# Splitting the loads of a large key/value cache over two queues, in place of sixteen tiny loads at the end

## The chip, the cores and the metric

The kernel runs on one core of a Trainium2 chip. The metric is the device time of one execution in microseconds (us), the median of the runs. The core's engines appear in the profile as PE (matrix multiplications; PEld is the loading of its stationary operand), DVE (vector work), ACT (scalar work, activations), POOL and SP (which here only issues transfers). Transfers between the large memory and the on-chip buffer are issued by SP or ACT and carried by 16 DMA engines that the core's queues share.

## What is computed

Two attention blocks for one new token, concatenated. Block A has 32 heads, each with its own keys and values over 32768 positions; block B has 32 query heads over 8 key/value heads and looks at the last 4096 positions only. All inputs are bf16.

```python
# A: x (1,1,512), k_cache and v_cache (1,32,32768,128), wq (512,4096), wo (4096,512)
q = (x @ wq) per head
scores = einsum("bhqd,bhkd->bhqk", q, k_cache) * 128 ** -0.5
p = softmax(scores)
o = einsum("bhqk,bhkd->bhqd", p, v_cache)
a = o @ wo
# B: the same with caches (1,8,32768,128), the last W = 4096 positions,
#    each key/value head used by four query heads
return concatenate([a, b], axis=-1)      # (1,1,1024)
```

A's caches are 2 x 268.4 MB; they are read once and make up 536.9 MB of the 570.4 MB that the kernel reads.

## The kernel before

The work is written as lists of operations, one list for each engine, with the waits between them derived from dependencies (`op`, `emit`). Each engine runs its own list in order. PE and DVE run the 32 heads of A as a loop of 16 passes of two heads; ACT and SP run theirs as straight code.

First come B's two groups of heads (`emit_qproj`, `emit_unit`, `emit_stats`, `emit_PT`, `emit_PV`), whose loads are 4 MB each. Then comes the loop over A's 32 heads (line 381). A head g does this:

- `load_k` (line 314) issues one load of 8 MB: 128 partitions, 64 KB each, into two of the three thirds of `kbuf`; the third of the thirds still holds keys of the head before. The load may start when PE has read the thirds it overwrites. The last head's keys come as two loads of 4 MB.
- `load_v` (line 327) issues one load of 8 MB into `vbuf`, which holds one head only. It may start when PE has finished the head before's product with the values (line 599).
- `emit_qcopy` (line 469): ACT copies the head's query into `qw`.
- `emit_unit` (line 473): PE transposes the keys in 32 batches (line 497), DVE copies each batch out (line 500), PE multiplies with the query (line 519). The first of these products needs `qw`.
- `emit_stats`: the maximum over the scores by DVE and PE, then the exponential on ACT (line 547).
- `emit_PT`: PE transposes the probabilities (line 571), ACT copies them (line 574) and copies a selector `hw` (line 577).
- `emit_PV`: PE multiplies with the values (line 599), and the result is gathered into `psG` (lines 613 to 626).

Every load of caches and weights is issued by SP through `load` (line 287), so they all stand in one queue, in the order in which SP's list has them: keys of head g, values of head g, keys of head g+1 and so on. Only the two loads of x (1 KB each, line 424) are issued by ACT, at the start.

After the last head SP issues the output weights: `kbuf<-wo`, two loads for B and five for A (line 392). Behind them it issues sixteen tiny loads (line 394): load i brings rows 0 to i, 16 bf16 values each, into the buffer `marks`, which nothing reads. Then come the output's two stores (line 668), and SP's list ends with waits for the sixteen tiny loads (line 399) and for the stores (line 401).

Of the kernel before, what the change touches and what calls it, by code (L numbers as in the profile page):

```python
# [3 lines left out]
BF16 = mybir.dt.bfloat16  # L4
# [5 lines left out]
DH = 128  # L10
NQH = 32
STRIPS = 4
HALF = 128
NT = 4
# [38 lines left out]
class _Kernel:  # L53
# [176 lines left out]
    def alloc(self):  # L230
        nc = self.nc
        sb = nc.alloc_sbuf_tensor
        self.kbuf = sb("kbuf", [128, 3 * HALF * DH], BF16)
        self.vbuf = sb("vbuf", [128, 2 * HALF * DH], BF16)
        self.kt = [sb(f"kt{i}", [128, 1024], BF16) for i in range(NKT)]
        self.psb = sb("psb", [128, 512], BF16)
        self.ptsb = sb("ptsb", [128, 512], BF16)
        self.ident = sb("ident", [128, 128], BF16)
        self.ones = sb("ones", [128, 128], BF16)
        self.e32 = sb("e32", [128, 32], F32)  # L240
        self.spread = sb("spread", [32, 4, 128], BF16)
        self.tr = {k: sb(f"tr_{k}", [128, 32], F32) for k in ("in", "a")}
        self.rows64 = sb("rows64", [128, 64], F32)
        self.nscale = sb("nscale", [1, 128], F32)
        self.m4 = sb("m4", [1, 128], F32)
        self.pb = sb("pb", [128, 512], F32)
        self.out_sb = sb("out_sb", [128, 512], BF16)
        self.marks = sb("marks", [16, 17 * 16], BF16)
        self.c = {}
        for name, d in self.X.items():  # L250
            HG = d["HG"]
            self.c[name] = dict(
                x=sb(f"x_{name}", [128, 4], BF16),
                oc=[sb(f"oc_{name}{i}", [128, DH + 1], F32) for i in range(2)],
                b=sb(f"b_{name}", [128, 32], F32),
                cm=sb(f"cm_{name}", [128, 32], F32),
                mr=sb(f"mr_{name}", [1, HG], F32),
                nb=sb(f"nb_{name}", [128, 2], F32),
                hot=sb(f"hot_{name}", [128, d["nb"]], F32),
                lh=sb(f"lh_{name}", [128, HG], F32),  # L260
                hsel=sb(f"hsel_{name}", [128, 64], F32),
                rinv=sb(f"rinv_{name}", [32, 1], F32),
                ob=sb(f"ob_{name}", [32, DH], BF16),
                oz=sb(f"oz_{name}", [128, 32], BF16),
            )

        self.qz = sb("qz", [128, 32 * self.X["B"]["NKVH"] + 64], BF16)
        self.qa = sb("qa", [128, NQH], BF16)
        self.qw = sb("qw", [128, 64], BF16)
        self.hw = sb("hw", [128, 32], F32)  # L270
        ps = nc.alloc_psum_tensor
        self.S = ps("psS", [128, 512], F32)
        self.T = [ps(f"psT{i}", [128, 512], F32) for i in range(NT)]
        self.PT = ps("psPT", [128, 512], F32)
        self.ACC = ps("psACC", [128, 512], F32)
        self.G = ps("psG", [128, 512], F32)
        s = nc.alloc_semaphore
        self.ksem = [s(f"ksem{i}") for i in range(2)]
        self.vsem = [s(f"vsem{i}") for i in range(2)]
        self.xsem = {n: s(f"xsem_{n}") for n in self.X}  # L280
        self.wosem = {n: [s(f"wosem_{n}{i}") for i in range(len(self.WO_CUTS[n]) - 1)] for n in self.X}
        self.outsem = {n: s(f"outsem_{n}") for n in self.X}
        self.marksem = [s(f"marksem{i}") for i in range(16)]

# [24 lines left out]
    def k_thirds(self, g):  # L311
        return (1, 0) if g % 2 == 0 else (1, 2)

    def load_k(self, g, parts):
        w = HALF * DH
        src = self.kv_src("k", "A", g)[:, 0, :]
        lo = min(self.k_thirds(g))
        free = [self.free["k"][t] for t in self.k_thirds(g)]
        if parts == 1:
            self.load(self.kbuf[:, w * lo:w * lo + 2 * w], src, self.mark("k", 0), *free)  # L320
            sem = self.mark("k", 1)
            self.op("sp", lambda e: e.sem_inc(sem, 16))
        else:
            for i, t in enumerate(self.k_thirds(g)):
                self.load(self.kbuf[:, w * t:w * t + w], src[:, w * (t - lo):w * (t - lo) + w], self.mark("k", i), *free)

    def load_v(self, g):
        self.load(self.vbuf[:, :], self.kv_src("v", "A", g)[:, 0, :], self.mark("v", 0), *self.free["v"])

    WQ_SLOT = {"B": 0, "A": 1}  # L330

# [20 lines left out]
    def plan(self):  # L352
        self.lsem = {"k": self.ksem, "v": self.vsem}
        self.fill = {w: [0, 0] for w in "kv"}
        self.free = {"k": [None] * 3, "v": [None] * 2}
        self.nbatch = 0
        self.copies = []
        self.pending = []
        self.psread = self.ptread = self.sread = self.accread = None
        self.gath = self.qcopy = self.hcopy = None  # L360
        self.constants()
        a, b = self.X["A"], self.X["B"]

        self.load_wq("B")
        self.load_b("k", 0)
        self.load_wq("A")
        self.load_b("k", 1)
        self.emit_qproj("B")
        self.emit_unit("B", 0)
        self.emit_qproj("A")  # L370
        self.emit_stats("B", 0)
        self.emit_unit("B", 1, {1: lambda: self.emit_PT("B", 0)})
        self.emit_stats("B", 1)
        for g in range(2):
            if g == 1:
                self.emit_PT("B", g)
            self.load_b("v", g)
            self.emit_PV("B", g)
        self.emit_spread("B")

        for g in range(NQH):
            self.loop = {"pe": g // 2, "dve": g // 2}
            self.load_k(g, 1 if g < NQH - 1 else 2)
            self.load_v(g)
            self.emit_qcopy(g)
            self.emit_unit("A", g)
            self.emit_stats("A", g)
            self.emit_PT("A", g)
            self.emit_PV("A", g)
        self.loop = {}  # L390
        for n in ("B", "A"):
            for part in range(len(self.WO_CUTS[n]) - 1):
                self.load_wo(n, part)
        for i in range(16):
            self.load(self.marks[0:i + 1, 16 * i:16 * i + 16], self.X["A"]["wo"][0:i + 1, 0:16], self.marksem[i])
        self.emit_spread("A")
        self.emit_proj()
        for i in range(16):
            self.op("sp", lambda e, i=i: e.wait_ge(self.marksem[i], 16))
        for n in ("B", "A"):  # L400
            self.op("sp", lambda e, n=n: e.wait_ge(self.outsem[n], 16))

# [70 lines left out]
    def emit_unit(self, name, g, hooks={}):  # L473

        d = self.X[name]
        thirds = (g,) if name == "B" else self.k_thirds(g)
        lo = min(thirds)
        order = [(t, i, 8 * (t - lo) + st) for i, t in enumerate(thirds) for st in range(8)]
        for n, (t, i, st) in enumerate(order):
            for half in range(2):  # L480
                self.emit_T(HALF * lo + 16 * st + 8 * half, self.landed("k", g if name == "B" else i), t)
            if n % 2:
                if n // 2 in hooks:
                    hooks[n // 2]()
                self.pending.append((name, g, order[n - 1][2], n == 1, n == len(order) - 1, self.nbatch - 4))
                if len(self.pending) > 1:
                    self.emit_S(self.pending.pop(0))

    def emit_T(self, tile, landed, third):
        b = self.nbatch  # L490
        self.nbatch += 1
        T, KT = self.T[b % NT][:, :].bitcast(BF16), self.kt[b % NKT]
        src = self.kbuf[:, DH * tile:DH * tile + 1024]
        def tr(e):
            inst = None
            for k in range(8):
                inst = e.transpose(T[:, 128 * k:128 * k + 128], src[:, DH * k:DH * k + DH], self.ident[:, :])  # L497
            return inst
        o = self.op("pe", tr, landed, self.copies[b - NT] if b >= NT else self.k_ident, to="dve")
        self.copies.append(self.op("dve", lambda v: v.tensor_copy(KT[:, :], T[:, :]), o, to="pe"))  # L500
        self.free["k"][third] = o

# [77 lines left out]
    def emit_PV(self, name, g):  # L580
        d, t = self.X[name], self.c[name]
        acc = self.ACC
        pt = self.ptsb[:, :].rearrange("p (j x) -> p j x", x=128)
        if name == "A":
# [3 lines left out]
            rows = 4  # L588
        else:
            w = HALF * DH  # L590
# [4 lines left out]
            rows = 16  # L595
        def mm(e):
# [2 lines left out]
                inst = e.matmul(acc[32 * c:32 * c + rows, 0:512], lhsT=lhsT, rhs=rhs, start=begin, stop=end,  # L599
                                tile_position=(0, 32 * c), skip_group_check=True)  # L600
            return inst
        pv = self.op("pe", mm, self.landed("v", 0 if name == "A" else g), self.ptread, self.accread, to="sp")
        for i in (0, 1) if name == "A" else (g,):
            self.free["v"][i] = pv

        pv = self.emit_gather(name, g, DH, DH + 1)
        oc = t["oc"][g % 2][:, 0:DH]
        o = None
# [101 lines left out]
```

## Time and profile before

| what | value |
|---|---|
| median of 2 runs | 1329.01 us (1328.94 to 1329.09) |
| the profiled execution | 1328.94 us; its span, first to last instruction, 1326.9 us |
| PE busy | 963.9 us, 73% |
| PEld busy | 678.1 us, 51% |
| DVE busy | 749.5 us, 56% |
| ACT busy | 54.8 us, 4% |
| moved by DMA | 570.66 MB, mean 430 GB/s |
| TensorE clock granted, mean | 0.839 of full speed |

Busy shares say how long an engine worked, not whether it set the end. The chain of waits, followed back from the last instruction, says what did. For transfers, the share of a queue is the time that its packets took, as a share of the time of 16 DMA engines. "Us to landing" is the time from a transfer's issue to its completion, and so includes what stood ahead of it.

### The profile page before, as it was taken

What the parts mean: (1) busy time and instruction counts of PE and PEld (TensorE: products, weight loads), DVE (VectorE), ACT (ScalarE), POOL (GpSimd) and SP (SyncE); (2) the same over time, 40 slices, a digit from 0 to 9 for tenths busy, and PEclk for the clock granted to TensorE, in tenths of its full rate; (3) what the DMA queues carried; (4) which work ended last, traced back from release to release, by engine and by line L of the source; (5) the groups of instructions that cost most, each with busy time, mean ns of one, the idle gap of its engine ahead of it and who ended that gap; (6) DMA issues with size and microseconds to landing.
All of it is one profiled execution on the core that took longest, in us unless ns stands there. A gap on an engine that the chain in (4) does not pass through costs nothing.

```text
span 1326.9 us, 28821 instructions
## 1 busy us (share of the span) xinstructions
PE 963.9 (73%) x13436; PEld 678.1 (51%) x13436; DVE 749.5 (56%) x1345; ACT 54.8 (4%) x167; POOL 2.3 (0%) x17
## 2 busy tenths in 40 slices
PE   3657678777667877766787777678777767877786
PEld 3544445554444555444465544446554444655453
DVE  3645466665456666545666645566664556666473
ACT  0000000000000000000000000000000000000000
POOL 0000000000000000000000000000000000000000
PEclk9877788887788888778888878888887888888798
DMA  9999999999999999999999999999999999999998
GB/s 393 431 433 436 432 431 435 437 429 433 441 429 433 435 435 431 433 441 429 433 435 435 431 433 441 427 435 435 433 433 433 437 431 435 435 431 435 433 435 341
DMA packets 13351, 570.66 MB, mean 430 GB/s; under 512 B 1812, under 2 KB 1816, under 8 KB 2200
## 3 DMA queue, kind: packets, MB, share of 16 engines
q1 hardware_dynamic: 13048, 570.44, 99.6%
q8 instruction: 12, 0.20, 0.1%
q10 hardware_dynamic: 288, 0.00, 0.0%
q14 instruction: 3, 0.02, 0.0%
HBM read 570.43 MB, written 0.00 MB: 430 GB/s over the span
## 4 chain that ended last, share of the span: by engine, by line
DMA 70%; PE 27%; DVE 1%; issue 0%; SPq 0%; ACT 0%
DMA kbuf<-in_A_k_cache_dram 65%; PE psT L497 23%; PE psS L519 4%; DMA kbuf<-in_B_k_cache_dram 3%; DMA kbuf<-in_A_wo_dram 3%; DVE kt L500 1%; PE psACC L599 0%; SPq L288 0%; DVE oc_A L615 0%; ACT psb L547 0%; DVE tr_in L536 0%; PE psPT L571 0%; ACT ptsb L574 0%; PE psPT L661 0%; PE psG L626 0%
## 5 line engine op out<-in xcount | busy, mean ns | idle before, releaser
L500 DVE COPY kt<-psT 128x1024 bf16<-128x1024 bf16 x1056 | 654.8, 683 | 245.3 <-PE psT L497 243.5
L497 PE MATMUL psT<-ident,kbuf 128*128 128x128 bf16 x8448 | 578.7, 234 | 176.7 <-DMA kbuf<-in_A_k_cache_dram 165.0
L497 PEld LDWEIGHTS psT<-ident,kbuf 128*128 128x128 bf16 x8448 | 539.3, 106 | 268.7 <-DMA kbuf<-in_A_k_cache_dram 173.1
L599 PE MATMUL psACC<-vbuf,ptsb 128*4 128x512 bf16 (+1 forms) x2112 | 182.9, 522 | 23.3 <-ACT ptsb L574 21.3
L519 PE MATMUL psS<-kt,qw 128*32 128x512 bf16 x2048 | 157.6, 385 | 15.4 <-DVE kt L500 15.4
L613 DVE TENSOR_SCALAR oc_A<-psACC,hot_A 128x128 f32<-128x128 f32 x32 | 11.2, 350 | 247.7 <-PE psG L626 247.7
L599 PEld LDWEIGHTS psACC<-vbuf,ptsb 128*4 128x4 bf16 (+1 forms) x2112 | 59.0, 110 | 137.8 <-issue 87.6
L547 ACT ACTIVATE psb<-psS,nb_A 128x512 bf16<-128x512 f32 x32 | 22.0, 687 | 1169.8 <-DVE nb_A L546 1169.8
L519 PEld LDWEIGHTS psS<-kt,qw 128*32 128x32 bf16 x2048 | 34.0, 95 | 57.9 <-DVE kt L500 31.3
L626 PE MATMUL psG<-oc_A,hw 128*32 128x128 f32 (+1 forms) x128 | 19.3, 227 | 52.3 <-DVE oc_A L615 52.3
L626 PEld LDWEIGHTS psG<-oc_A,hw 128*32 128x32 f32 x128 | 11.4, 109 | 62.5 <-DVE oc_A L615 55.0
L571 PE MATMUL psPT<-ident,psb 128*128 128x128 bf16 x136 | 18.0, 274 | 34.0 <-ACT psb L547 34.0
L615 DVE SCALAR_TENSOR_TENSOR oc_A<-psACC,hot_A,oc_A 128x128 f32<-128x128 f32 x96 | 33.7, 351 | 3.4
L536 DVE TENSOR_REDUCE tr_in<-psS 128x1 f32<-128x512 f32 x34 | 23.5, 692 | 17.1 <-PE psS L519 17.1
L571 PEld LDWEIGHTS psPT<-ident,psb 128*128 128x128 bf16 x136 | 10.1, 117 | 37.1 <-ACT psb L547 36.7
L540 PE MATMUL psACC<-rows,tr_in 128*1 128x64 f32 x64 | 8.7, 217 | 25.5 <-DVE tr_in L536 25.5
L574 ACT ACTIVATE ptsb<-psPT 128x512 bf16<-128x512 bf16 x34 | 20.3, 597 | 28.3 <-PE psPT L571 28.3
L540 PEld LDWEIGHTS psACC<-rows,tr_in 128*1 128x1 f32 x64 | 2.7, 81 | 35.1 <-DVE tr_in L536 35.1
L544 PE MATMUL psACC<-mr_A,nscale 1*128 1x1 f32 x64 | 12.1, 256 | 9.7 <-DVE mr_A L543 9.7
L544 PEld LDWEIGHTS psACC<-mr_A,nscale 1*128 1x128 f32 x64 | 9.4, 182 | 15.7 <-DVE mr_A L543 15.7
L546 DVE COPY nb_A<-psACC 128x1 f32<-128x1 f32 x32 | 5.1, 158 | 15.0 <-PE psACC L544 15.0
L543 DVE TENSOR_REDUCE mr_A<-psACC 1x1 f32<-1x64 f32 x32 | 6.8, 213 | 11.7 <-PE psACC L540 11.7
(71 smaller groups left out, 75.0 us busy)
## 6 DMA issues: line engine op xcount, KB each, us to landing
kbuf<-in_B_k_cache_dram SPq DMA_DIRECT2D x2, 4096.0 KB, 32.3
vbuf<-in_B_v_cache_dram SPq DMA_DIRECT2D x2, 4096.0 KB, 23.9
kbuf<-in_A_k_cache_dram SPq DMA_DIRECT2D x2, 4096.0 KB, 22.0
vbuf<-in_B_wq_dram SPq DMA_DIRECT2D x1, 4096.0 KB, 12.3
vbuf<-in_A_wq_dram SPq DMA_DIRECT2D x1, 4096.0 KB, 32.2
kbuf<-in_B_wo_dram SPq DMA_DIRECT2D x2, 2048.0 KB, 33.1
kbuf<-in_A_wo_dram SPq DMA_DIRECT2D x1, 1408.0 KB, 28.5
kbuf<-in_A_wo_dram SPq DMA_DIRECT2D x1, 1024.0 KB, 30.8
```

Source lines behind the costliest of these rows:

```text
L497: inst = e.transpose(T[:, 128 * k:128 * k + 128], src[:, DH * k:DH * k + DH], self.ident[:, :])
L500: self.copies.append(self.op("dve", lambda v: v.tensor_copy(KT[:, :], T[:, :]), o, to="pe"))
L519: inst = e.matmul(self.S[32 * c:32 * c + 32, :], lhsT=win, rhs=self.kt[(bb + c // 2) % NKT][:, 512 * (c % 2):512 * (c % 2) + 512], start=b ...
L536: o = dve(lambda v: v.reduce_max(tr["in"][:, 0:1], self.S[:, :], axis=AXX), self.sdone, self.k_pool, to="pe" if name == "A" else None)
L540: o = self.op("pe", lambda e: e.matmul(self.ACC[0:1, 0:64], lhsT=tr["in"][:, 0:1], rhs=self.rows64[:, :], start=True, stop=True, skip_grou ...
L544: o = self.op("pe", lambda e: e.matmul(self.ACC[:, 64:65], lhsT=self.nscale[:, :], rhs=t["mr"][0:1, :], start=True, stop=True, skip_group_ ...
L547: self.sread = self.op("act", lambda s: s.activation(out=self.psb[:, :], in_=self.S[:, :], func=ACTF.Exp, bias=t["nb"][:, k:k + 1], scale= ...
L571: inst = e.transpose(PT[:, 128 * jj:128 * jj + 128], self.psb[:, 128 * jj:128 * jj + 128], self.ident[:, :])
L574: self.ptread = self.op("act", lambda s: s.activation(out=self.ptsb[:, :], in_=PT[:, 0:512], func=ACTF.Copy), self.psread, to="pe")
L599: inst = e.matmul(acc[32 * c:32 * c + rows, 0:512], lhsT=lhsT, rhs=rhs, start=begin, stop=end, tile_position=(0, 32 * c), skip_group_check ...
L615: o = self.op("dve", lambda v, src=src, hot=hot: v.scalar_tensor_tensor(out=oc, in0=src, scalar=hot, in1=oc, op0=ALU.mult, op1=ALU.add), p ...
L626: return self.op("pe", lambda e: e.matmul(self.G[0:32, c0 + c:c0 + c2], lhsT=win, rhs=t["oc"][g % 2][:, c:c2], start=False, stop=True, ski ...
```

## The change

Sixteen tiny loads, their buffer, their semaphores and the waits for them are taken out. Each load of A's keys and values is split by partitions: SP loads partitions 0 to 63, ACT loads partitions 64 to 127, with 64 KB in each partition as before. ACT's half waits for a count (`relay`) that SP raises right after it has issued its own half, so it needs no other wait. The halves have semaphores of their own, and PE waits for both. In ACT's list the keys of head g+1 are issued behind the query copy of head g and ahead of its exponential; the values of head g+1 behind the copies of `emit_PT` and ahead of the query copy of head g+1. B's loads and all weights stay whole on SP's queue.

```diff
@@ load_k, load_v
-    def load_k(self, g, parts):
+    def load_half(self, queue, which, g, pieces, *deps):
+        src = self.kv_src(which, "A", g)[:, 0, :]
+        rows, n = (slice(0, 64), 0) if queue == "sp" else (slice(64, 128), 1)
+        if queue == "act":
+            deps = [(self.relay[which], g + 1)]
+        for part, dst, a, b in pieces:
+            sem = self.vsem[n] if which == "v" else self.kasem[part][n]
+            self.op(queue, lambda e, dst=dst, a=a, b=b, sem=sem: e.dma_start(dst[rows, :], src[rows, a:b]).then_inc(sem, 16), *deps)
+        if queue == "sp":
+            self.op("sp", lambda e: e.sem_inc(self.relay[which], 1))
+
+    def load_k(self, queue, g):
         w = HALF * DH
-        src = self.kv_src("k", "A", g)[:, 0, :]
         lo = min(self.k_thirds(g))
-        free = [self.free["k"][t] for t in self.k_thirds(g)]
-        if parts == 1:
-            self.load(self.kbuf[:, w * lo:w * lo + 2 * w], src, self.mark("k", 0), *free)
-            sem = self.mark("k", 1)
-            self.op("sp", lambda e: e.sem_inc(sem, 16))
+        if g < NQH - 1:
+            pieces = [(0, self.kbuf[:, w * lo:w * lo + 2 * w], 0, 2 * w)]
+            if queue == "sp":
+                for sem in self.kasem[1]:
+                    self.op("sp", lambda e, sem=sem: e.sem_inc(sem, 16))
         else:
...
+            pieces = [(i, self.kbuf[:, w * t:w * t + w], w * (t - lo), w * (t - lo) + w) for i, t in enumerate(self.k_thirds(g))]
+        self.load_half(queue, "k", g, pieces, *[self.free["k"][t] for t in self.k_thirds(g)])
+
+    def load_v(self, queue, g):
+        self.load_half(queue, "v", g, [(0, self.vbuf[:, :], 0, 2 * HALF * DH)], *self.free["v"])
@@ the loop over A's heads
-            self.load_k(g, 1 if g < NQH - 1 else 2)
-            self.load_v(g)
+            self.load_k("sp", g)
+            self.load_v("sp", g)
+            if g == 0:
+                self.load_k("act", g)
+                self.load_v("act", g)
             self.emit_qcopy(g)
             self.emit_unit("A", g)
+            if g < NQH - 1:
+                self.load_k("act", g + 1)
             self.emit_stats("A", g)
             self.emit_PT("A", g)
             self.emit_PV("A", g)
+            if g < NQH - 1:
+                self.load_v("act", g + 1)
@@ behind the loads of output weights, and at the end
-        for i in range(16):
-            self.load(self.marks[0:i + 1, 16 * i:16 * i + 16], self.X["A"]["wo"][0:i + 1, 0:16], self.marksem[i])
         self.emit_spread("A")
         self.emit_proj()
-        for i in range(16):
-            self.op("sp", lambda e, i=i: e.wait_ge(self.marksem[i], 16))
@@ emit_unit: PE's wait for keys (emit_PV has the like for values)
-                self.emit_T(HALF * lo + 16 * st + 8 * half, self.landed("k", g if name == "B" else i), t)
+                self.emit_T(HALF * lo + 16 * st + 8 * half,
+                            [self.landed("k", g)] if name == "B" else [(s, 16 * (g + 1)) for s in self.kasem[i]], t)
```

More of the change, by code (lines that the diff above doesn't have):

```diff
@@ L247, in alloc @@
         self.out_sb = sb("out_sb", [128, 512], BF16)
-        self.marks = sb("marks", [16, 17 * 16], BF16)
         self.c = {}
@@ L279, in alloc @@
         self.vsem = [s(f"vsem{i}") for i in range(2)]
+        self.kasem = [[s(f"kasem{i}{j}") for j in range(2)] for i in range(2)]
+        self.relay = {w: s(f"relay_{w}") for w in "kv"}
         self.xsem = {n: s(f"xsem_{n}") for n in self.X}
@@ L282, in alloc @@
         self.outsem = {n: s(f"outsem_{n}") for n in self.X}
-        self.marksem = [s(f"marksem{i}") for i in range(16)]
     def load(self, dst, src, sem, *deps):
@@ L312, in k_thirds @@
         return (1, 0) if g % 2 == 0 else (1, 2)
-    def load_k(self, g, parts):
+    def load_half(self, queue, which, g, pieces, *deps):
[9 more added lines that the diff above has]
+    def load_k(self, queue, g):
         w = HALF * DH
-        src = self.kv_src("k", "A", g)[:, 0, :]
         lo = min(self.k_thirds(g))
-        free = [self.free["k"][t] for t in self.k_thirds(g)]
-        if parts == 1:
-            self.load(self.kbuf[:, w * lo:w * lo + 2 * w], src, self.mark("k", 0), *free)
-            sem = self.mark("k", 1)
-            self.op("sp", lambda e: e.sem_inc(sem, 16))
-        else:
[L324 to L328, printed above, removed]
+        if g < NQH - 1:
[3 more added lines that the diff above has]
+                    self.op("sp", lambda e, sem=sem: e.sem_inc(sem, 16))
+        else:
+            pieces = [(i, self.kbuf[:, w * t:w * t + w], w * (t - lo), w * (t - lo) + w) for i, t in enumerate(self.k_thirds(g))]
+        self.load_half(queue, "k", g, pieces, *[self.free["k"][t] for t in self.k_thirds(g)])
+    def load_v(self, queue, g):
+        self.load_half(queue, "v", g, [(0, self.vbuf[:, :], 0, 2 * HALF * DH)], *self.free["v"])
     WQ_SLOT = {"B": 0, "A": 1}
@@ L498, in tr @@
             return inst
-        o = self.op("pe", tr, landed, self.copies[b - NT] if b >= NT else self.k_ident, to="dve")
+        o = self.op("pe", tr, *landed, self.copies[b - NT] if b >= NT else self.k_ident, to="dve")
         self.copies.append(self.op("dve", lambda v: v.tensor_copy(KT[:, :], T[:, :]), o, to="pe"))
@@ L601, in mm @@
             return inst
-        pv = self.op("pe", mm, self.landed("v", 0 if name == "A" else g), self.ptread, self.accread, to="sp")
+        landed = [self.landed("v", g)] if name == "B" else [(s, 16 * (g + 3)) for s in self.vsem]
+        pv = self.op("pe", mm, *landed, self.ptread, self.accread, to="sp")
         for i in (0, 1) if name == "A" else (g,):
```

## Prediction

> **What bounds the kernel now.** I read the page's slices, queues and chain first.
>
> ```profile
> DMA  9999999999999999999999999999999999999998
> GB/s 393 431 433 436 432 431 435 437 429 433 441 429 433 435 435 431 433 441 429 433 435 435 431 433 441 427 435 435 433 433 433 437 431 435 435 431 435 433 435 341
> q1 hardware_dynamic: 13048, 570.44, 99.6%
> ...
> q10 hardware_dynamic: 288, 0.00, 0.0%
> ...
> DMA 70%; PE 27%; DVE 1%; issue 0%; SPq 0%; ACT 0%
> ```
>
> The 16 DMA engines are busy in every slice. SP's queue q1 moves nearly all; q10, ACT's, carries only the two x. PE stands in the chain with 27%, but only between the release of a buffer and the next load's issue, while q1 still works on an earlier load. So transfers set the end, and PE, DVE and ACT (73%, 56%, 4% busy) do not.
>
> The timeline shows the margins around one values load and the next head:
>
> ```profile
> 1194.61 0.22 ACT L577 ACTIVATE hw<-hsel_A 128x32 f32<-128x32 f32 x1
> 1194.72 0.20 ACT L470 ACTIVATE qw<-qa 128x1 bf16<-128x1 bf16 x1
> ...
> 1199.51 0.33 SPq L288 DMA_DIRECT2D vbuf<-in_A_v_cache_dram  x1
> ...
> 1207.20 5.36 PE L497 MATMUL psT<-ident,kbuf 128*128 128x128 bf16 x64 [5.67 <-DMA kbuf<-in_A_k_cache_dram]
> ...
> 1212.49 0.61 PE L519 MATMUL psS<-kt,qw 128*32 128x512 bf16 x8
> ```
>
> Columns: start, length, what, the idle time before. The values load is issued 7.7 us before the head's keys have landed (1207.20 - 1199.51), so the queue is never empty. The transposes of head 0 begin at 83.52 and those of head 30 at 1245.91: 1162.4 / 30 = 38.75 us a head, 16.78 MB in it, 433 GB/s. 32 heads are 1240 us; the rest of the span, 87 us, is B, the weights and the tail.
>
> Last, what happens where two queues meet on the engines: the landing times at the start, then the queues' shares between 100 and 160 us and between 60 and 160 us.
>
> ```profile
> vbuf<-in_B_wq_dram SPq DMA_DIRECT2D x1, 4096.0 KB, 12.3
> ...
> x_B<-in_B_x_dram ACTq DMA_DIRECT2D x1, 1.0 KB, 6.3
> x_A<-in_A_x_dram ACTq DMA_DIRECT2D x1, 1.0 KB, 12.9
> ```
> ```profile
> q1 hardware_dynamic: 448, 25.69, 99.2%
> q8 instruction: 5, 0.08, 0.6%
> ```
> ```profile
> q1 hardware_dynamic: 851, 43.41, 100.6%
> q8 instruction: 6, 0.10, 0.4%
> ```
>
> x_A, 1 KB on ACT's queue, takes as long as 4 MB on SP's beside it: two queues share the same engines in turns, row by row, and a second queue is no second set of engines. In the last fences q1 moves 25.69 MB in 99.2% of 16 x 60 us, 27.0 GB/s for each engine. q8, the only other queue with packets of size, moves 0.08 MB in 0.6% of it, 5.8 us: 13.9 GB/s, 1.94 times slower; over 100 us, 0.10 MB in 6.4 us, 1.73 times slower.
>
> **The change part by part.** *The tiny loads* (16 issues, 136 rows of 32 bytes): their issue keeps SP busy from 1290.9 to 1310.8, but the next thing on SP, the first store, is issued at 1318.65. At the end SP waits 0.5 us, for the store's landing and not for them. Removed: 0 to -0.5 us.
>
> *SP's side.* 65 issues of 0.33 us stay, with half the rows, behind the same waits; semaphore increments are added behind them. *ACT's side.* 65 new issues. ACT's own two took 0.39 and 0.46 us, so some 28 us, on an engine that is busy 55 us. The keys' issue falls into ACT's idle time ahead of the exponential (1169.8 us in all; for head 0 SP issues at 94.46 and the exponential runs at 107.46). The values' issue makes the following `qw` copy wait for SP: it moves from 1194.72 to about 1199.51 + 0.33 + 0.46 + 0.1 = 1200.4, and PE needs it at 1212.49: 12 us of cover (4.7 us in the last head, where SP issues at 1277.63 and the product starts at 1283.33). What PE needs from ACT for the values' product, the copies at L574 and L577, stands ahead of the new wait. Price 0; without cover some 0.9 us a head, 28 us.
>
> *ACT's half comes later* than SP's by 0.33 + 0.46 = 0.8 us. The queue then holds 6 to 8 us of other rows, so 0; with an empty queue 64 x 0.8 = 51 us. *First load*: its ACT half takes turns with B's last values (8 KB rows on SP's queue). 4 rows of 64 KB per engine at 2.4 us delay these values by up to 9.7 us and the next values' issue from 67.6 to 77.3, still before the first keys land at 83.5. Price 0. *Tail*: a lag of one row, 2.4 us, may pass into the last values' landing; PE's four waits for A's output weights, 2.1 us in all, hide most of it. 0 to +2.4 us.
>
> *The rows themselves* are the open term. Each half goes to 64 partitions, and the halves' rows meet on each engine from two queues. No row shows a sizable load to fewer than 128 partitions, nor two queues with sizable rows for long. From below: same bytes, same engines, 0. A gain is bounded by the queue's own best slice, 441 against 433 GB/s: -22 us. From above: a half takes as long as a whole load, 1240 us more. The nearest row is q8's: packets of another queue between q1's, slower by 1.73 to 1.94, say 1.84. Its weakness: few packets, and not bound for these buffers. If ACT's half alone pays this, A takes 1240 x (0.5 + 0.5 x 1.84) = 1761 us; if both halves do, 1240 x 1.84 = 2282. I can't tell these apart and take the middle, 2021. The queues stay filled meanwhile, since keys are issued 11 us after the keys before have landed (94.46 - 83.52), before slower values could land. Sum: 2021 + 87 = 2108 us of span; the profiled execution was 2.0 us longer than its span and is within 0.1 us of the median: 2110.
>
> [...]
>
> **The rivals.** *Turns without loss* (the other side, not slower): each engine alternates between the halves, every row keeps its 27.0 GB/s, and 433 GB/s stays. For it: x_A's turns, and shares at 100% in the windows with q8's packets. It decides if SP's and ACT's rows on different engines are spread over the buffer's two halves at each moment. Price: the -0.5 to +2.4 us above and, as an allowance that no row sizes, up to 5 us for the completions of 65 more loads and -2 us for what I overlook: 1329, 1326 to 1336. *The lag opens a gap*: rows keep their pace, but each ACT half meets an empty queue; 51 us, 1380. Against it: 6 to 8 us of cover; it decides only once that falls under 0.8. *Faster*: 2% is 26.6 us, and the -22 us above doesn't reach it. That ACT's half stays on SP's queue is excluded: x on q10 shows ACT's own.
>
> **How the numbers follow.** Rows slowed 0.60 (its own range 1850 to 2570: one half at 1.84 up to both as long as a whole); turns without loss 0.33; gaps 0.05; faster 0.02. I put the slowing first since the only sizable packets from a second queue ran at nearly half pace; the full shares of q1 beside them keep the rival alive. The likeliest gives 2110. The range needs both: 1326 to 2570. A difference under 2% can't be told from no change: faster 0.02, within 2% 0.33, slower 0.65.
>
> **What would show it.** q1 and q10 each with some 270 MB. Slowed rows: slices near 215 to 305 GB/s with engines still 9 tenths busy, heads 55 to 78 us apart (1761 / 32 and 2480 / 32), longer waits of PE for keys and now for values at L599, and a chain nearly all DMA. Turns without loss: 433 GB/s and 38.75 us a head. Gaps: slices of 415 GB/s, engines idle at each issue. `qw` late would show as PE waiting at L519 for ACT. The prediction is wrong if heads stay at 38.75 us, or if ACT's or SP's order, not the pace of rows, sets them.

## The result and the profile after

| | before | changed |
|---|---|---|
| median of 2 runs | 1329.01 us | 2435.43 us (2418.74 to 2452.11) |
| ratio | | 1.8325, 95% interval 1.7785 to 1.8865 |
| profiled execution, its span | 1328.94, 1326.9 us | 2452.11, 2450.1 us |
| moved by DMA, mean | 430 GB/s | 233 GB/s |
| TensorE clock granted, mean | 0.839 | 0.682 |

The page's slices and queues of the changed kernel. The page cuts the span into 40 equal slices; the row DMA has the busy share of the engines in tenths, the row GB/s what they moved; a queue's row has packets, MB and share:

```profile
DMA  9999999999999999999999999999999999999997
GB/s 404 223 217 214 217 214 216 214 216 219 213 216 220 214 220 223 220 226 236 233 241 246 249 243 247 261 242 221 234 243 255 218 223 229 232 234 239 233 231 218
...
q1 hardware_dynamic: 8616, 302.00, 51.6%
q10 hardware_dynamic: 5488, 268.44, 48.1%
```

The DMA engines are as busy as before and carry about half as much a second, 233 GB/s against 430. A "9" in the row DMA stands over 404 GB/s in the first slice and over 213 to 261 in those behind it; only the row GB/s says what it is worth. The first slice, which holds B with its whole loads, still runs at 404.

The queues' shares between 100 and 160 us, the stretch in which q1's rows ran at 27.0 GB/s for each engine before:

```profile
q1 hardware_dynamic: 128, 7.27, 56.7%
q10 hardware_dynamic: 120, 5.77, 44.7%
```

7.27 MB in 56.7% of 16 x 60 us is 13.4 GB/s, 5.77 MB in 44.7% is 13.4 as well. Either queue's rows run at half pace.

PE's wait for keys in the kernel before, and then the longest waits of the changed kernel (engine, what waited, for what: us in all, times, longest):

```profile
PE psT L497 <- DMA kbuf<-in_A_k_cache_dram: 165.0, 31, 13.0
```

```profile
ACT psb L561 <- DVE nb_A L560: 1730.8, 32, 66.8
DVE kt L514 <- PE psT L511: 1008.9, 159, 36.8
...
PE psT L511 <- DMA kbuf<-in_A_k_cache_dram: 926.5, 33, 36.0
...
ACT qw L483 <- SPq L323: 539.5, 32, 20.7
...
PE psACC L613 <- DMA vbuf<-in_A_v_cache_dram: 360.4, 32, 18.8
```

PE waits 926.5 us for keys (165.0 before) and 360.4 us for A's values, for which it didn't wait before. Together that is 1122 us more, and the span grew by 1123 us. ACT's `qw` waits 539.5 us for SP, and nothing waits for it, as the timeline of one head shows:

```profile
228.37 5.86 PE L613 MATMUL psACC<-vbuf,ptsb 128*4 128x512 bf16 x64 [3.29 <-DMA vbuf<-in_A_v_cache_dram]
...
234.28 0.47 SPq L321 DMA_DIRECT2D vbuf<-in_A_v_cache_dram  x1
...
234.82 0.47 ACTq L321 DMA_DIRECT2D vbuf<-in_A_v_cache_dram  x1
235.34 0.21 ACT L483 ACTIVATE qw<-qa 128x1 bf16<-128x1 bf16 x1 [9.51 <-SPq L323]
...
267.60 5.09 PE L511 MATMUL psT<-ident,kbuf 128*128 128x128 bf16 x64 [31.31 <-DMA kbuf<-in_A_k_cache_dram]
...
272.62 0.61 PE L533 MATMUL psS<-kt,qw 128*32 128x512 bf16 x8
```

SP issues its half at 234.28, ACT its own 0.54 us later, `qw` is copied at 235.34, and PE needs it 37 us later. The page's own chain says nothing here: followed back from the end it stops after 14 us, inside the tail. So the forecast "a chain nearly all DMA" stays open, and the waits above stand in its place.

### The profile page after: what moved, and what is told of

It reads as the page before. It is cut to its first block, busy times and chain, and to the rows that moved or that the text cites. A ratio compares the mean times of both kernels' runs of the same rounds, so it can differ in the third digit from the quotient of the medians.

```text
span 2450.1 us, 29036 instructions
## 1 busy us (share of the span) xinstructions
PE 972.4 (40%) x13436; PEld 684.8 (28%) x13436; DVE 749.4 (31%) x1345; ACT 58.4 (2%) x167; POOL 2.3 (0%) x17
## 2 busy tenths in 40 slices
DMA packets 14121, 570.68 MB, mean 233 GB/s; under 512 B 2580, under 2 KB 2584, under 8 KB 2968
## 5 line engine op out<-in xcount | busy, mean ns | idle before, releaser
L511 PE MATMUL psT<-ident,kbuf 128*128 128x128 bf16 x8448 | 578.7, 234 | 939.0 <-DMA kbuf<-in_A_k_cache_dram 926.5
L613 PE MATMUL psACC<-vbuf,ptsb 128*4 128x512 bf16 (+1 forms) x2112 | 189.4, 536 | 364.0 <-DMA vbuf<-in_A_v_cache_dram 360.4
L613 PEld LDWEIGHTS psACC<-vbuf,ptsb 128*4 128x4 bf16 (+1 forms) x2112 | 64.2, 112 | 479.8 <-issue 461.4
L483 ACT ACTIVATE qw<-qa 128x1 bf16<-128x1 bf16 x32 | 6.6, 206 | 539.5 <-SPq L323 539.5
```

## The experiments

Three theories, all of them conjectures, stood at the start. S: a load to 64 neighbouring partitions lands in one half of the receiving buffer, and that halves the pace. Q: rows of two queues slow each other. L: twice as many loads, or ACT's later issue, cost the time.

**Split by columns.** Same queues, relays and number of loads; only the cut is another.

```diff
-        rows, n = (slice(0, 64), 0) if queue == "sp" else (slice(64, 128), 1)
+        n = 0 if queue == "sp" else 1
...
+            h = (b - a) // 2
+            dst, a = dst[:, n * h:n * h + h], a + n * h
```

> The same two queues, the same number of loads, waits and relays as the changed kernel, but each load is split by columns: SP brings the first 32 KB of all 128 partitions, ACT the other 32 KB of all 128. Theory S (a load to 64 partitions reaches only half of the buffer's receiving side, and engines that write to the same half at the same moment share its pace): every row keeps its pace, so heads stay at 38.75 us, slices at 433 GB/s, and the time is 1326 to 1336 us. Theory Q (large rows of two queues slow each other on an engine, whatever they are bound for): heads near 73 us and 2350 to 2500 us, as with the change. Theory L (twice as many loads, or ACT's later issue, cost it): also 2350 to 2500 us.

Measured 1334.65 us (1334.55 to 1335.72, 4 runs), ratio to the kernel before 1.0042 (1.0027 to 1.0058). Its slices and queues:

```profile
GB/s 388 426 431 419 435 428 434 431 431 434 430 434 430 434 429 433 431 432 433 432 433 429 435 428 434 432 433 432 431 433 429 435 430 432 433 432 432 431 430 357
...
q1 hardware_dynamic: 12776, 302.00, 52.9%
q10 hardware_dynamic: 9648, 268.44, 46.8%
```

Each queue carries what it carries in the changed kernel, to the digit, at full pace. Q, for rows of 32 KB, and L fall. At most 0.4% is left of them.

**Both halves on one queue.** SP issues partitions 0 to 63 and then 64 to 127; ACT issues nothing.

```diff
+            for n, rows in enumerate((slice(0, 64), slice(64, 128))):
...
-                self.load_k("act", g + 1)
```

> The same halves by partitions, both issued by SP one behind the other, nothing on ACT. Theory S: at each moment all engines write to the same 64 partitions, in step and with nothing to pull them apart, so 210 to 220 GB/s from the first head to the last, two times 1240 us for the 32 heads and 2540 to 2580 us in all, somewhat slower than the changed kernel. Theory Q: no second queue, so 433 GB/s and 1326 to 1336 us. Theory L (number of loads): 2350 to 2500 us.

Measured 2667.28 us. The halves alone are enough; a second queue isn't needed for the loss. The busy times and rates of this run by stretch (start and end in us; the last three numbers are the granted clock, the DMA share and GB/s) show no change over the run:

```profile
100.00:1000.00 900.00, 325.27 (x4407) 231.66 (x4408) 249.53 (x434) 17.45 (x55) 0.00 (x0) 0.66 1.00 208
1000.00:2600.00 1600.00, 583.38 (x8024) 411.03 (x8022) 452.50 (x791) 31.71 (x100) 0.00 (x0) 0.67 1.00 209
```

It is slower by 87 us than the upper end of my range, 2580, and 208 GB/s lies just under the 210 to 220 I had expected.

**Even and odd partitions.** One edit to the changed kernel:

```diff
-        rows, n = (slice(0, 64), 0) if queue == "sp" else (slice(64, 128), 1)
+        rows, n = (slice(0, 128, 2), 0) if queue == "sp" else (slice(1, 128, 2), 1)
```

> The changed kernel with one edit: SP brings the even partitions, ACT the odd ones, 64 each as before, so that either half spans the whole range 0 to 127. Theory S in its plain form (what counts is which part of the buffer a load spans as a whole): 433 GB/s and 1326 to 1340 us. [...] Theory Q: 2350 to 2500 us.

Measured 1331.85 us (one run), 432 GB/s between 100 and 1200 us:

```profile
100.00:1200.00 1100.00, 818.02 (x11296) 575.33 (x11292) 636.43 (x1113) 49.03 (x144) 0.00 (x0) 0.84 1.00 432
```

64 partitions a load, 64 KB a row, two queues, and a loss of some 0.2%. The plain form of S holds, and Q falls for rows of 64 KB too. So it is neither the number of partitions nor the number of rows for an engine, but where the partitions lie.

**The tiny loads alone.** The kernel before without its sixteen tiny loads and the waits for them.

> The kernel before without its sixteen tiny loads, their buffer and the waits for them; the cache's loads whole and on SP's queue. All theories: 0 to 0.5 us less than the kernel before, so 1328.5 to 1329.1 us; if the tiny loads had held the end, up to 2 us less.

Measured 1329.56 us (1329.13 to 1329.89, 11 runs) against 1329.25 (15 runs), ratio 1.0002 (0.9993 to 1.0011). They cost nothing that can be measured; the time lies 0.5 us above the upper end of my range, 1329.1, less than the 0.8 us over which its runs spread.

**Source or destination.** Keys and values may stand on any partition as long as both use the same. So the reading and the receiving pattern can be exchanged separately: halves into the buffer from alternate rows of memory, and alternate partitions of the buffer from halves of memory.

```diff
+        halves = (slice(64 * n, 64 * n + 64), slice(n, 128, 2))
+        to, fro = halves[0], halves[1]
...
-            self.op(queue, lambda e, dst=dst, a=a, b=b, sem=sem: e.dma_start(dst[rows, :], src[rows, a:b]).then_inc(sem, 16), *deps)
+            self.op(queue, lambda e, dst=dst, a=a, b=b, sem=sem: e.dma_start(dst[to, :], src[fro, a:b]).then_inc(sem, 16), *deps)
```

The second run has `to` and `fro` the other way round.

> The changed kernel with the source's rows exchanged: partitions 0 to 63 (SP) get the even rows of keys and of values, partitions 64 to 127 (ACT) the odd rows. Which row a key stands on doesn't matter to attention as long as its value stands on the same; nothing is left out. So the buffer sees the change's halves and the large memory sees the pattern of the even-odd run. Theory D (the slowing is at the buffer that receives): 2350 to 2600 us, rows at half pace, slices of 210 to 260 GB/s. Theory H (it is at the memory that is read: engines that read 2 MB apart meet): 433 GB/s and 1328 to 1340 us.

> The counterpart: the even partitions (SP) get rows 0 to 63 of keys and values, the odd ones (ACT) rows 64 to 127. The large memory sees the change's halves, the buffer the even-odd pattern. Theory D: 433 GB/s and 1328 to 1340 us. Theory H: 2350 to 2600 us.

Measured 2522.07 us and 1331.51 us. The first has the rates of the change, the second those of the kernel before; their slices in this order:

```profile
GB/s 409 213 212 213 214 216 214 216 214 208 217 215 216 216 218 217 226 216 216 218 218 229 233 251 270 235 233 236 231 238 230 219 218 232 219 212 216 214 207 208
```
```profile
GB/s 388 433 434 409 435 424 436 436 434 430 436 432 432 436 436 428 434 436 436 430 434 434 436 430 436 432 436 432 434 434 432 432 438 432 432 434 438 432 430 342
```

The loss is at the buffer that receives.

**Out of step.** The changed kernel has both halves of the buffer in use by two queues, so why don't the halves add up? A possible answer: the engines take turns between the queues in step, so all of them write to the same half at the same moment. In the packets' records of the changed kernel they do so at first: sixteen rows of q10 start between 120.0 and 123.9 us, sixteen of q1 between 124.7 and 128.7. Small loads that occupy only some engines should then help, once, by putting those engines behind.

```diff
+    def lag(self, queue):
+        src = self.kv_src("k", "A", 1)[:, 0, :]
+        for i in range(2):
+            if queue == "sp":
+                dst, n = self.kbuf[slice(64 + i, 96 + i, 4), 2 * HALF * DH:2 * HALF * DH + 16384], 16384
+            else:
+                dst, n = self.pad[0:8, 4 * i:4 * i + 4], 4
...
+            self.op(queue, lambda e, dst=dst, n=n, i=i: e.dma_start(dst, src[0:8, 0:n]).then_inc(self.lagsem[queue][i], 16))
...
+            if g == 0:
+                self.lag("sp")
```

> The changed kernel plus four small loads, once: behind head 0's keys SP issues two loads of 8 rows of 32 KB (into a part of the keys' buffer that is free then), and ACT, at the same place in its queue, two loads of 8 rows of 8 bytes. They occupy eight of the 16 engines, and put these one 64 KB row behind the other eight, with the two queues' turns still matched. Theory D8 (engines that write to the same place stand in the two groups of eight, and they lose because they do so at the same moments): from there on one group writes to one half of the buffer while the other writes to the other half, and the rows run at full pace: heads at 38.75 us from head 1 on, 1335 to 1400 us, if the groups don't drift into step again. If half of the partners drift back: up to 1900 us. Theory D1 (partners stand in the same group of eight, or what a load spans decides, in step or not): no change, 2400 to 2480 us.

> The control of the run before it: the same four loads with 16 rows each, so that all 16 engines are put one row behind. Theory D8 and theory D1 alike: no engine is moved against another, 2400 to 2570 us. Were it fast, the small loads would act through something other than the engines' steps.

Measured 2538.34 us and, for the control, 2602.48 us, 58 and 32 us above the ranges I had given for no change. The lag was there: in the packets' records of the first run, eight rows of q1 start between 111.1 and 114.7 us and eight of q10 between 111.7 and 114.9, so both queues' rows run at once. Yet each still takes 4.8 to 5.0 us, where a 64 KB row at 27.0 GB/s takes 2.4. The rates of the run with the lag by stretch:

```profile
130.00:1000.00 870.00, 328.54 (x4483) 230.80 (x4482) 253.95 (x444) 18.75 (x56) 0.00 (x0) 0.67 1.00 215
1000.00:2400.00 1400.00, 529.11 (x7200) 373.17 (x7200) 404.74 (x706) 32.18 (x95) 0.00 (x0) 0.67 1.00 223
```

D8 falls. The changed kernel's own packets say the same, without a lag. From 100 us on 7937 of its 64 KB rows start. For 959 of them, on average at least 14 of the 16 or so rows in flight were bound for the same half; these took 5.08 us in the median. For 3850 only 6 to 10 were, the row itself counted, and these took 4.57. An even use of the two halves is worth a tenth, and not a factor of two.

I then supposed that the engines that hinder each other stand in pairs within a group of eight (theory N), and meant loads of 15, 13, ... 1 rows to stagger the two of each pair:

```diff
+        for i, k in enumerate((15, 13, 11, 9, 7, 5, 3, 1)):
+            if queue == "sp":
+                n = HALF * DH
+                dst = self.kbuf[slice(i, 8 * k + i - 7, 8), 2 * n:3 * n]
```

> The changed kernel plus sixteen small loads, once, behind head 0's keys: SP issues eight loads of 15, 13, 11, 9, 7, 5, 3 and 1 rows of 32 KB, ACT at the same place eight of 15 to 1 rows of 8 bytes. [...] Theory T (what a load spans as a whole decides, in step or not): 2400 to 2620 us.

> The control of the run before it: the same sixteen loads at the same places, all with 16 rows, so that every engine is put eight rows of 32 KB behind and none against another. Theory N and theory T alike: 2450 to 2630 us.

Measured 2523.89 us, and 2489.37 us for the control. No gain, so these loads did not help as N wanted it. That tells against N only if they staggered the pairs as I meant, and this was not shown: no record tells which engine moves which row of a load.

**Quarters.** Loads of 32 partitions, two for each queue: neighbours first (0 to 31 and 32 to 63 on SP, 64 to 95 and 96 to 127 on ACT), then alternate partitions within a half.

```diff
+            for p in (rows.start, rows.start + 32):
+                quarter = slice(p, p + 32)
```
```diff
+            for p in (rows.start, rows.start + 1):
+                quarter = slice(p, rows.stop, 2)
```

> [...] Theory T with the two halves of the buffer as the places (0 to 63 and 64 to 127): as with the change, 2400 to 2620 us. [...]

> The quarters once more, but each of alternate partitions within a half: SP loads the even partitions of 0 to 63 and then the odd ones, ACT the same of 64 to 127. Again 32 partitions a load and two loads a queue. Theory T (a load whose partitions all lie in one half of the buffer moves at half pace, however they lie there): 2400 to 2620 us, slices of 205 to 240 GB/s. Theory A (neighbouring partitions in one load are what costs, and alternate ones are free, as in the even-odd run): 433 GB/s and 1330 to 1345 us.

Measured 2577.1 and 2615.01 us. Their rates up to 1000 us, in this order:

```profile
100.00:1000.00 900.00, 337.90 (x4596) 241.47 (x4597) 261.10 (x453) 18.68 (x55) 0.00 (x0) 0.67 1.00 212
```
```profile
100.00:1000.00 900.00, 337.05 (x4559) 240.37 (x4560) 259.07 (x449) 18.68 (x55) 0.00 (x0) 0.67 1.00 212
```

32 neighbours are little worse than 64 (217 GB/s in the same stretch of the changed kernel), and leaving every second partition out is no better as long as the load stays in one half. Theory T fits all runs: a load that lies within partitions 0 to 63 or within 64 to 127 ran at half pace (208 to 217 GB/s up to 1000 us), one that spans both at full pace (431 to 433 up to 1200).

The slow kernels differ among themselves (2419 to 2667 us). The changed kernel's own two runs lie 33 us apart, and the other slow kernels were run once each, so I read nothing into differences of a few per cent between them.

## Why the prediction was right, and where not

The forecast was 2110 us, between 1326 and 2570, slower at 0.65. The time is 2435 us; the case that came is the one forecast, and its size was off by 325 us. The range held the rival's time as well, so lying inside it says little.

- **The bound** was read right: transfers set the end before and after. PE's added waits for keys and values account for the added span.
- **The open term was mis-sized.** The step "I can't tell these apart and take the middle, 2021" failed. Both queues' rows pay, not one's: 13.4 GB/s each. The transposes of head 0 begin at 110.49 us and those of head 30 at 2320.97: 73.7 us a head, 2358 us for 32. Beside the 2021 I took that is 337 us more; beside the 2282 of the end "if both halves do", 76 us. The price itself, 1.84 times, was near: 73.7 / 38.75 = 1.90. The range's upper end took a half to last as long as a whole load, my estimate, which no row of before sized; the run with both halves on one queue, 2667.28 us, lies above it.
- **The reason behind the price was wrong.** It came from q8's packets, as a cost of sizable rows from a second queue. The column split shows that a second queue with rows of 32 KB costs 0.4%, the even-odd split that one with rows of 64 KB costs 0.2%. That q8's packets run at half pace has to have another cause, which no run here shows; its nearness is luck.
- **Turns without loss** was to be decided by whether the engines' rows are spread over the two halves at each moment. They were for nearly half of the changed kernel's rows (3850 of 7937), and these gained a tenth (4.57 against 5.08 us), far from the 2.4 us of a row at 27.0 GB/s.
- **The lag, SP's and ACT's sides, `qw`**: price 0 held as far as it shows. SP's issue grew from 0.33 to 0.47 us, ACT's took 0.47. The even-odd run has the same issues and the same order and is 2.6 us longer than the kernel before, so all of these together cost some 2.6 us at most. The up to 5 us allowed in the prediction for the completions of 65 more loads no run shows apart.
- **First load**: wrong in its course. ACT's first half was issued at 64.12, 8.5 us behind SP's at 55.62, because ACT's list has B's exponential (60.24) and copy (64.11) ahead of it. The next values went out at 71.4, not at 77.3, and PE got the first keys at 110.49 and not at 83.5, by the pace of the rows.
- **The tiny loads**: 0 to -0.5 us was forecast; measured is no difference.

Left open: why the two halves don't add up when both are in flight. The 214 to 217 GB/s of most early slices with two queues are hardly more than 208 with one; over the whole span it is 233 against 214 (570.7 MB in 2665.3 us). The simple answer, engines in step, fell by the lag and by the packets' records. Open too is where the border lies: no run loads 64 neighbouring partitions across the middle, 32 to 95, so the runs don't tell the two halves as such from the distance between a load's first and last partition.

## What to carry to other kernels

Cut a large load by columns or by alternate partitions, and keep every load spread over both halves of the partitions; a cut into 0 to 63 and 64 to 127 cost a factor of 1.9 in transfer time on two queues (73.7 against 38.75 us a head) and of 2.1 on one (208 against 433 GB/s). With the engines busy throughout, a second queue gained nothing here: the cuts that did no harm gave 1331.85 and 1334.65 us against 1329.25, and no version tried here beats the kernel before. Before looking for waits, divide the megabytes by the engine time in the queue's row: 13.4 against 27.0 GB/s showed at once that the rows themselves were slow, where "busy" showed nothing.

## What the runs showed of the hardware that I had not expected

- Pace followed the span of each single load over the partitions, and what was in flight together only by a tenth (4.57 against 5.08 us a row): 32 or 64 partitions within a half, neighbours or alternate, on one queue or two, in step or lagged, all ran at 205 to 240 GB/s for most of the run; 64 alternate partitions over both halves at 432.
- The slow pace isn't steady. The changed kernel starts, behind the first slice, at 214 to 223 GB/s, climbs to 261 in its 26th slice and falls back to 221 two slices later; the run from alternate rows into halves climbs to 270. The run on one queue stays between 205 and 214 in all slices but the first and the last. What lets the two queues' rows drift into a somewhat better pace, and out of it, wasn't found.
- Rows of 32 KB in place of 64 KB cost little: the column split has 22441 packets where the even-odd split has 14121, and takes 2.8 us longer (1334.65 and 1331.85).
